# A fused joint network, forward and backward: another order for the row units and the second data gradient, and two gelu passes held behind the first GH product

## The chip, the cores and the metric

The kernel runs on one core of a Trainium2 chip. The metric is the device time of one execution in microseconds, the median of several runs. TensorE (PE in the profile) multiplies matrices and writes its results to PSUM; VectorE (DVE), ScalarE (ACT) and GpSimd (POOL) work on tiles in SBUF, the first two in PSUM too; SyncE (SP) and GpSimd issue the DMAs of this kernel. Each engine takes its instructions in the order of its own queue. An instruction whose input, or whose output buffer, is not yet free waits, and all that stand behind it in that queue wait with it.

## The reference

The forward pass is two convolutions of three taps with stride 2 and a gelu each, and then a joint network:

```python
h  = gelu(conv3(x,  w1))[:, ::2]        # x: (2, 16000, 256)
f  = gelu(conv3(h,  w2))[:, ::2]        # f: (2, 4000, 256)
j  = tanh((f @ w_f)[:, :, None] + (g @ w_g)[:, None])   # (2, 4000, 8, 256)
out = j @ w_o                           # (2, 4000, 8, 256)
```

All tensors are bfloat16. The kernel returns `out` and, for a given `grad_out` of the same shape, the gradients of `x`, `w1`, `w2`, `g`, `w_f`, `w_g` and `w_o`.

## The kernel before

The 4000 positions of both batch rows, with a gap between them, are laid side by side as 8016 columns and cut into 16 tiles of 512 columns, the last one shorter. For each tile `n` the outer loop runs four steps of the joint network, with two of the eight `u` in each. A step (`joint_units`, the "main" work) is, for each `u`: a square of the tanh on ScalarE (JSQ), matmuls of the output gradient with `w_o` (L623), and a VectorE pass on their result (NGZ, L627), which GpSimd adds up over the `u` (ACCN, L646); then blocks of output matmuls (L690), which ScalarE copies out (OUT, L692), alternating with matmuls of the gradient of `w_o` (L729).

Between the units of the main work, `weave` puts units of "fill" work, at a fixed ratio (0.92 fill units for each main unit). The fill is one chain of generators, written out by hand in the list `parts`. While tile `n` is in its joint steps, the fill holds the front of tile `n + 1` and the back of tile `n - 1`:

- `conv_units(n + 1)`: the first convolution, for even and for odd positions (L320), and the first four operations of each gelu: a square on ScalarE (`g_sq`), a VectorE pass (`g_s`, "the first pass" below), a sigmoid on ScalarE, and the VectorE product that writes HT. These four go into the queue `later`; `weave` takes two of them for each main unit (`pump`).
- `d1_units(n - 1)`: the gradient GF of the second gelu's input (L424, L426).
- `row_units(n - 1)`: five units, which transpose tiles on TensorE (L460) and copy them out (L462): first NGFE, copied by VectorE, and then four sets of HT and GF rows, copied by ScalarE. The next bullet's matmuls read them.
- `gwf_units` and `gw2_units(n - 1)`: the gradients of `w_f` (L506) and `w2` (L524) and their sums on VectorE (L408).
- `d5_units(n - 1)`: the data gradient of the second convolution, four units: two for even positions (two matmuls each, L447) and two for odd ones (four matmuls each). VectorE multiplies each result by G1 and writes GH (L450).
- then `ghr_units`, `conv2_units`, `e_units` and `fe_units`, which transpose GH, run the second convolution, form the gradients of `x` and `w1`, and start the next tile's joint network.

All matmul results and transposes of these units share one PSUM pool, `psp`, of 7 buffers. So a unit's matmuls wait until an engine has emptied the buffer that they are given. The order on each engine is made by the tile framework's scheduler from the order in which the units are issued, from its own estimates of time, and from dependencies added by hand. One of these is the list `held`: an operation that is put into `held` gets a dependency on the next GH product (L453), so that VectorE does it behind that product. Before, this held the last of the four gelu operations of the odd positions, for tiles `n > 1`; its line in the profile is L328.

Of the kernel before, what the change touches and what calls it, by code (L numbers as in the profile page):

```python
# [32 lines left out]
def kernel(  # L33
# [30 lines left out]
    def geom(n):  # L64
        c0 = n * CW
        return c0, min(CW, L - c0)
# [26 lines left out]
    def nsets(n):  # L93
        return 4 if geom(n)[1] == CW else 3

    def sets(n):
        s = nsets(n)
        return [(k, geom(n)[1] // s) for k in range(s)]
# [28 lines left out]
    def ps_f32():  # L127
        return psp.tile([P, 512], FP32, name="ps", tag="ps")
# [125 lines left out]
    held = []  # L254
    NOSYNC = mybir.DependencyInfo(mybir.DependencyClass.NoSync, mybir.DependencyReason.DATA)

    def pump(k):
        for _ in range(k):
            if later:
                later.popleft()()  # L260
# [37 lines left out]
    def conv_units(n):  # L298
        c0, W = geom(n)
        seconds = []  # L300
        st = S[n]
        HT = htp.tile([P, 2, KT, CW + 2], BF16, name="HT")
        G1 = g1p.tile([P, 2, KT, CW + 2], BF16, name="G1")
        st["HT"], st["G1"] = HT, G1
        if n == G - 1:
            nc.gpsimd.memset(G1[:, 0, :, 2 + W:3 + W], 0.0)
        if n == 0:
            nc.gpsimd.memset(HT[:, 1, :, 1:2], 0.0)
            nc.gpsimd.memset(G1[:, 1, :, 1:2], 0.0)
        else:  # L310
            nc.gpsimd.tensor_copy(out=HT[:, 1, :, 1:2], in_=S[n - 1]["HT"][:, 1, :, CW + 1:CW + 2])
        taps = {0: ((1, 0, 0), (2, 1, 0), (0, 3, -1)), 1: ((0, 1, 0), (2, 3, 0), (1, 2, 0))}
        for par in range(2):
            xb = gel.tile([P, KT, CW], BF16, name="g_x")
            for mt in range(KT):
                ps = ps_f32()
                k = 0
                for (i, c, sh) in taps[par]:
                    for kt in range(KT):
                        nc.tensor.matmul(ps[:, :W], lhsT=W1[:, i, kt, mt * P:(mt + 1) * P],  # L320
                                         rhs=st["X", c][:, kt, 16 + sh:16 + sh + W], start=(k == 0), stop=(k == 5))
                        k += 1
                nc.scalar.copy(out=xb[:, mt, :W], in_=ps[:, :W])  # L323
                yield
            first, second = gelu(xb, W, HT[:, par], G1[:, par], 2, HALVES if n == 0 else ((0, KT),))
            if par == 1 and n > 1:
                mult = first.pop()
                first.append(lambda: held.append(mult()))  # L328
            later.extend(first)
            seconds += second  # L330
            if n == 0:
                pump(len(first))
        seconds0.extend(seconds)
        if n > 0:
            seconds0.append(lambda: nc.gpsimd.tensor_copy(out=G1[:, 1, :, 1:2],
                                                          in_=S[n - 1]["G1"][:, 1, :, CW + 1:CW + 2]))
# [67 lines left out]
    def flush(key, acc, ps):  # L404
        if first_flush[key]:
            nc.vector.tensor_copy(out=acc, in_=ps)
        else:
            nc.vector.tensor_tensor(out=acc, in0=acc, in1=ps, op=ALU.add)  # L408
# [21 lines left out]
    def d5_units(n):  # L430
        st = S[n]
        c0, W = geom(n)
        N = W + 1 if n == G - 1 else W
        GF, G1 = st["GF"], st["G1"]
        GH = ghp.tile([P, 2, KT, CW + 4], BF16, name="GH")
        st["GH"] = GH
        if n == 0:
            nc.gpsimd.memset(GH[:, 0, :, 1:2], 0.0)
        else:
            nc.gpsimd.tensor_copy(out=GH[:, 0, :, 1:2], in_=S[n - 1]["GH"][:, 0, :, CW + 1:CW + 2])  # L440
        for par, taps in ((0, ((1, 0),)), (1, ((2, -1), (0, 0)))):
            for mt in range(KT):
                ps = ps_f32()
                k, last = 0, len(taps) * KT - 1
                for (i, sh) in taps:
                    for kt in range(KT):
                        nc.tensor.matmul(ps[:, :N], lhsT=W2T[:, i, kt, mt * P:(mt + 1) * P],  # L447
                                         rhs=GF[:, kt, 2 + sh:2 + sh + N], start=(k == 0), stop=(k == last))
                        k += 1
                gh = nc.vector.tensor_tensor(out=GH[:, par, mt, 2:2 + N], in0=ps[:, :N],  # L450
                                             in1=G1[:, par, mt, 2 - par:2 - par + N], op=ALU.mult)
                while held:
                    tc.add_manual_dep(held.pop().ins, gh.ins.name, NOSYNC, reason="held")  # L453
                yield
# [9 lines left out]
    def load_fr(n):  # L464
        W = geom(n)[1]
        FR = frp.tile([P, KT, 4, P], BF16, name="FR")
        nb = len(blocks(W))
        for kt in range(KT):
            nc.sync.dma_start_transpose(out=FR[:, kt, 0:nb, :], in_=S[n]["FT"][:, kt, 0:nb * P])
        S[n]["FR"] = FR  # L470
# [42 lines left out]
    def gw2_units(n):  # L513
        W = geom(n)[1]
        HG = S[n]["HG"]
        for i in (1, 2, 0):
            ps = ps_f32()
            for k, M in sets(n):
                for dt in range(KT):
                    if i == 0:  # L520
                        lhsT = HG[0][:M, 6 + dt, :] if k == 0 else HG[k - 1][:M, 2 + dt, :]
                    else:
                        lhsT = HG[k][:M, (0 if i == 1 else 2) + dt, :]
                    nc.tensor.matmul(ps[:, dt * D:(dt + 1) * D], lhsT=lhsT,  # L524
                                     rhs=HG[k][:M, 4:6, :].rearrange("p k d -> p (k d)"),
                                     start=(k == 0 and dt == 0), stop=(k == nsets(n) - 1 and dt == KT - 1))
            flush("2", ACC2[:, i, :], ps[:])
            yield
        first_flush["2"] = False

    def alternate(a, b):
        gens = [a, b]
        while gens:
            gen = gens.pop(0)
            if next(gen, StopIteration) is not StopIteration:
                gens.append(gen)
                yield
# [196 lines left out]
    def chain(*gens):  # L734
        for gen in gens:
            yield from gen

    def empty(k):
        for _ in range(k):
            yield  # L740
# [83 lines left out]
    for n in range(G):  # L824
        back, fwd = n > 0, n + 1 < G
        conv = conv_units(n + 1) if fwd else iter(())
        conv2 = conv2_units(n + 1) if fwd else iter(())
        late_open[0] = False
        parts = []
        if back:  # L830
            d1, e, rows, ghr = d1_units(n - 1), e_units(n - 1), row_units(n - 1), ghr_units(n - 1)
            parts += [islice(conv, 2), islice(d1, 1), islice(conv, 1), d1, conv, alternate(rows, d5_units(n - 1)),
                      gwf_units(n - 1), gw2_units(n - 1), islice(ghr, 1), islice(conv2, 1), ghr, conv2, islice(e, 6)]
            if fwd:
                parts.append(fe_units(n + 1))
            parts.append(e)
        else:
            parts += [conv, empty(3), islice(conv2, 1), empty(3), conv2, empty(3), fe_units(n + 1)]
        fill = chain(*parts)
        ratio = (0.92 if n > 0 else 0.4) if n + 1 < G else 0.72  # L840
        for up in range(U // 2):
            step = n * (U // 2) + up
            for i in range(2):
                if 2 * step + 4 + i < len(order):
                    load_got(*order[2 * step + 4 + i])
            if step + 1 < len(orderp):
                load_go(*orderp[step + 1])
            if up == 1:
                load_fr(n)
            if back and up < 2:  # L850
                load_xr(n - 1, 2 * up)
                load_xr(n - 1, 2 * up + 1)
            main = joint_units(n, up)
            weave(main, fill, ratio)
            if up == U // 2 - 1:
                for _ in fill:
                    pump(2)
                    pump_late(1)
                pump(len(later))
                late_open[0] = True  # L860
                pump_late(len(late))
            for i in range(2):
                if 2 * step + 2 + i < len(order):
                    tanh(*order[2 * step + 2 + i])
            if step + 1 < len(orderp):
                load_jr(*orderp[step + 1])
            if n + 2 < G:
                load_x(n + 2, ((0, 1, 3, 2)[up],))
    n = G - 1
# [79 lines left out]
```

## Time and profile before

| | |
|---|---|
| median of 3 runs | 850.34 us (848.83 to 851.24) |
| the profiled execution's own time | 843.12 us |
| its span in the profile | 841.4 us |
| PE busy | 812.8 us, 97% |
| ACT busy | 678.4 us, 81% |
| DVE busy | 620.3 us, 74% |
| POOL busy | 394.6 us, 47% |
| granted TensorE clock, mean | 0.994 |

In the rows of the profile, an engine's wait is written as the waiting instruction, an arrow, and the instruction that released it, then the total in us, how often, and the longest. A row of the timeline is the start in us from the span's start, the time taken, the engine, the line, the operation with its output and inputs, and in brackets the engine's idle time just before and what ended it. Instructions of one kind that follow each other are merged to one row with their count. Matmuls overlap: a group's time in the row is longer than the distance to the next group's start, so distances between starts are used for TensorE; and VectorE and ScalarE rows overlap by about 0.1 us with the next.

### The profile page before, as it was taken

Reading aid. Unit: us, or ns where it says so; the run is one execution under the profiler, and the core shown is the slowest. Engines: PE = TensorE matmul, PEld = TensorE weight load, DVE = VectorE, ACT = ScalarE, POOL = GpSimd, SP = SyncE. Lnnn points to the kernel's source line nnn. Section 1 sums busy time; section 2 is a strip of 40 time slices with the busy share of each in tenths; the row PEclk is TensorE's granted clock in tenths of the full one; section 3 lists DMA queues with packets and bytes.
Section 4 is the critical chain, followed back from the end, with each engine's and each line's share of the span. In section 5 each row is a group of like instructions: output and inputs, shape, how many; then the busy total and the mean of one; then the engine's idle time right before and its main releaser. Section 6 shows DMA issues by size and latency. Waiting matters only on the chain.

```text
span 841.4 us, 17055 instructions
## 1 busy us (share of the span) xinstructions
PE 812.8 (97%) x6396; PEld 598.2 (71%) x6396; DVE 620.3 (74%) x1217; ACT 678.4 (81%) x1080; POOL 394.6 (47%) x423
## 2 busy tenths in 40 slices
PE   7969999999999999999999999999999999999997
PEld 3546677767768677676766777677686776878796
DVE  4896696876778767697866968768687676967644
ACT  3889998796978969699796987969789696987744
POOL 1154544444534535444486644445345354445661
PEclk9999999999999999999999999999999999999999
DMA  9988999999999999999999999999999999999954
GB/s 188 194 198 182 212 229 233 216 251 235 225 221 259 226 229 245 243 222 183 224 255 210 233 233 228 251 210 265 238 237 264 210 227 231 220 210 228 243 157 135
DMA packets 398515, 187.21 MB, mean 223 GB/s; under 512 B 346464, under 2 KB 382200, under 8 KB 398432
## 3 DMA queue, kind: packets, MB, share of 16 engines
q1 hardware_dynamic: 378112, 119.00, 77.9%
q0 software_dynamic: 20320, 67.12, 27.5%
q8 instruction: 50, 0.82, 0.4%
q14 instruction: 33, 0.27, 0.1%
HBM read 51.38 MB, written 50.34 MB: 121 GB/s over the span
## 4 chain that ended last, share of the span: by engine, by line
PE 43%; ACT 41%; DVE 6%; issue 5%; DMA 4%; POOL 0%; SPq 0%; ACTq 0%; POOLq 0%; DVEq 0%
ACT JT L396 12%; PE ps L593 7%; ACT OUT L692 6%; ACT JSQ L617 6%; PE GWO_ps L729 6%; PE ps L580 6%; PE ps L690 6%; ACT rows L462 5%; PE ps L355 5%; PE ps L524 4%; PE ps L623 4%; ACT g_s L260 3%; ACT g_x L323 3%; PE pst L460 2%; ACT GX L583 2%
## 5 line engine op out<-in xcount | busy, mean ns | idle before, releaser
L646 POOL TENSOR_TENSOR ACCN<-ACCN,NGZ 128x1024 f32<-128x1024 f32 (+1 forms) x80 | 168.7, 2109 | 69.1 <-DVE NGZ L627 68.0
L627 DVE SCALAR_TENSOR_TENSOR NGZ<-JSQ,ps 128x512 bf16<-128x512 bf16 (+3 forms) x272 | 167.5, 640 | 43.2 <-PE ps L623 39.9
L692 ACT CAST OUT<-ps 128x512 bf16<-128x512 f32 (+1 forms) x252 | 148.4, 600 | 58.4 <-PE ps L690 58.2
L396 ACT ACTIVATE JT<-FE,GE 128x512 bf16<-128x512 f32 (+3 forms) x272 | 182.3, 711 | 4.0 <-PE ps L623 1.9
L617 ACT ACTIVATE JSQ<-JT 128x1024 bf16<-128x1024 bf16 (+1 forms) x128 | 135.8, 1064 | 25.6 <-DVE NGZ L627 25.6
L729 PE MATMUL GWO_ps<-GO,JR 128*128 128x256 bf16 (+1 forms) x1008 | 148.6, 273 | 2.1 <-DVE JR L462 2.1
L690 PE MATMUL ps<-WO,JT 128*128 128x256 bf16 (+1 forms) x1008 | 148.7, 274 | 0.3 <-ACT rows L462 0.3
L717 POOL DMA_DIRECT2D out_dram<-OUT x76 | 55.8, 735 | 184.4 <-ACT OUT L692 171.5
L623 PE MATMUL ps<-GOT,WOT 128*128 128x512 bf16 (+1 forms) x512 | 139.2, 376 | 0.8 <-DVE rows L462 0.8
L260 DVE SCALAR_TENSOR_TENSOR g_s<-g_sq,g_x 128x1024 bf16<-128x1024 bf16 (+2 forms) x49 | 81.2, 1657 | 50.1 <-ACT g_sq L260 50.1
L729 PEld LDWEIGHTS <-JR 128*128 128x128 bf16 (+1 forms) x1008 | 96.9, 98 | 28.6 <-DVE JR L462 2.4
L690 PEld LDWEIGHTS <-JT 128*128 128x128 bf16 (+1 forms) x1008 | 97.9, 98 | 22.1 <-issue 1.6
L580 PE MATMUL ps<-W1T,GH 128*128 128x256 bf16 (+2 forms) x756 | 100.4, 273 | 0.0
L408 DVE TENSOR_TENSOR ACC<-ACC,ps 128x512 f32<-128x512 f32 x90 | 61.5, 684 | 44.5 <-PE ps L524 32.8
L580 PEld LDWEIGHTS <-GH 128*128 128x128 bf16 (+2 forms) x756 | 83.5, 116 | 13.0
L320 PE MATMUL ps<-XC,W 128*128 128x512 bf16 (+1 forms) x384 | 91.3, 375 | 1.1 <-DMA XC<-in_x_dram 1.1
L593 PE MATMUL ps<-rows,XR 128*128 128x256 bf16 (+1 forms) x756 | 90.4, 273 | 0.0
L593 PEld LDWEIGHTS <-XR 128*128 128x128 bf16 (+1 forms) x756 | 74.0, 98 | 11.6
L583 ACT CAST GX<-ps 128x512 bf16<-128x512 f32 (+2 forms) x126 | 72.2, 587 | 10.5 <-DMA out_dram<-GX 4.1
L241 POOL DMA_DIRECT2D out_dram<-GX x67 | 36.7, 548 | 82.1 <-ACT GX L583 75.0
L623 PEld LDWEIGHTS <-WOT 128*128 128x128 bf16 x512 | 48.5, 98 | 33.6 <-issue 2.3
L320 PEld LDWEIGHTS <-W 128*128 128x128 bf16 x384 | 37.4, 98 | 38.5 <-issue 1.4
(131 smaller groups left out, 1214.2 us busy)
## 6 DMA issues: line engine op xcount, KB each, us to landing
GO<-in_grad_out_dram SPq DMA_DIRECT2D x56, 512.0 KB, 5.3
out_dram<-OUT POOLq DMA_DIRECT2D x56, 512.0 KB, 5.5
out_dram<-GX POOLq DMA_DIRECT2D x55, 256.0 KB, 4.3
XR<-in_x_dram POOLq DMA_DIRECT2D x39, 256.0 KB, 6.3
XR<-in_x_dram POOLq DMA_DIRECT2D x13, 320.0 KB, 6.2
GOT<-in_grad_out_dram SPq DMA_TRANSPOSE x136, 5.7
JR<-JT SPq DMA_TRANSPOSE x128, 4.8
GO<-in_grad_out_dram SPq DMA_DIRECT2D x4, 384.0 KB, 5.0
```

What stands on the lines that cost most here:

```text
L260: later.popleft()()
L320: nc.tensor.matmul(ps[:, :W], lhsT=W1[:, i, kt, mt * P:(mt + 1) * P], rhs=st["X", c][:, kt, 16 + sh:16 + sh + W], start=(k == 0), stop=(k ...
L396: nc.scalar.activation(out=JT[:, mt, lo:hi], in_=S[n]["FE"][:, mt, lo:hi], func=ACT.Tanh, bias=GE[:, b, mt, u:u + 1], scale=1.0)
L580: nc.tensor.matmul(ps[:M, cj * D:(cj + 1) * D], lhsT=GH[:, par, kt, o:o + s * (M - 1) + 1:s], rhs=W1T[:, i, kt, :], start=(j == 0), stop=( ...
L593: nc.tensor.matmul(ps[:, dt * D:(dt + 1) * D], lhsT=XR[:M, 4 * k + i + 2 * (1 - par), dt * P:(dt + 1) * P], rhs=t[:M, g + 2 * par:g + 2 * ...
L617: nc.scalar.activation(out=JSQ[:, :, :W], in_=JT[:, :, :W], func=ACT.Square)
L623: nc.tensor.matmul(ps[:, :W], lhsT=WOT[:, kt, mt * P:(mt + 1) * P], rhs=GOT[:, kt, :W], start=(kt == 0), stop=(kt == KT - 1))
L627: nc.vector.scalar_tensor_tensor(out=NGZ[:, mt, lo:hi], in0=JSQ[:, mt, lo:hi], scalar=1.0, in1=ps[:, lo:hi], op0=ALU.subtract, op1=ALU.mul ...
L646: st["last"] = nc.gpsimd.tensor_tensor(out=out, in0=in0, in1=st["NGZ", u][:, :, :W], op=ALU.add)
L690: nc.tensor.matmul(ps[:M, j * V:(j + 1) * V], lhsT=st["JT", u][:, kt, o:o + M], rhs=WO[:, kt, :], start=(kt == 0), stop=(kt == KT - 1))
L692: nc.scalar.copy(out=OUT[:M, k, :], in_=ps[:M, :])
L729: nc.tensor.matmul(GWO_ps[:, dt, :], lhsT=JR[:M, j, dt, k, :], rhs=GO[:M, k, j * V:(j + 1) * V], start=(n_gwo[0] == 0), stop=(n_gwo[0] == ...
```

## The change

The change has two parts. Inside the loop, `alternate(rows, d5)` issues the row units R and the units D of the data gradient in turn: R D R D R D R D R. The new function `braid` issues R D R D R D R R D: the last set of rows now comes before the last unit of the data gradient. The call behind the loop, for the last tile, still uses `alternate`.

The second part is in the odd positions' gelu: of the four operations, the second (the first VectorE pass) and the fourth (the product that writes HT) are put into `held`, where before only the fourth was. Both appear as L328 in the changed kernel. Lines from `alternate` on are 4 higher there.

```diff
@@ conv_units
             if par == 1 and n > 1:
-                mult = first.pop()
-                first.append(lambda: held.append(mult()))
+                for j in (1, 3):
+                    first[j] = partial(lambda f: held.append(f()), first[j])
             later.extend(first)
@@ behind gw2_units
+    def braid(rows, d5):
+        for gen in (rows, d5, rows, d5, rows, d5, rows, rows, d5):
+            yield next(gen, None)
+
@@ the loop over tiles
-            parts += [islice(conv, 2), islice(d1, 1), islice(conv, 1), d1, conv, alternate(rows, d5_units(n - 1)),
+            parts += [islice(conv, 2), islice(d1, 1), islice(conv, 1), d1, conv, braid(rows, d5_units(n - 1)),
                       gwf_units(n - 1), gw2_units(n - 1), islice(ghr, 1), islice(conv2, 1), ghr, conv2, islice(e, 6)]
```

## The prediction

> **What bounds the kernel now.** I read the page's first part, then TensorE's longest waits, then the busy time of each engine inside one tile, and last the timeline of the stretch where TensorE stands still.
>
> ```profile
> span 841.4 us, 17055 instructions
> PE 812.8 (97%) x6396; PEld 598.2 (71%) x6396; DVE 620.3 (74%) x1217; ACT 678.4 (81%) x1080; POOL 394.6 (47%) x423
> ```
> ```profile
> PE ps L524 <- ACT rows L462: 5.3, 13, 0.7
> PE ps L447 <- DVE GH L450: 3.9, 11, 0.7
> ```
> ```profile
> core 0: us, PE busy (x) PEld busy (x) DVE busy (x) ACT busy (x) POOL busy (x), PEclk, DMA share, GB/s
> 335.04:346.20 11.16, 10.49 (x89) 7.28 (x87) 8.75 (x18) 11.13 (x16) 6.08 (x7) 1.00 1.06 263
> 346.30:385.80 39.50, 39.50 (x309) 29.61 (x307) 30.72 (x68) 31.17 (x59) 17.01 (x18) 1.00 1.12 212
> ```
>
> TensorE is the bound. Only two waits recur on it once per tile, and both lie in the stage that the change edits. The windows are one tile period: the stage (335.04 to 346.20) has 0.67 us without matmuls, the rest of the period none; there PE is busy 39.50 of 39.50 us at full clock. In the stage ScalarE is busy 11.13 of 11.16 us, so there ScalarE, not TensorE, may set the pace. What can be won lies in these stages, and what is won there is kept, since nothing outside them is late.
>
> The stage on TensorE. I call the four GH matmul groups D1 to D4 (L447), the transposes of the four row sets R1 to R4 (L460), their ScalarE copies by the same names, and the next two output blocks O1 and O2 (L690):
>
> ```profile
> 338.00 1.03 PE L623 MATMUL ps<-GOT,WOT 128*128 128x512 bf16 x4
> 339.29 1.03 PE L447 MATMUL ps<-GF,W2T 128*128 128x512 bf16 x4 [0.26 <-DVE GH L450]
> 340.15 0.59 PE L623 MATMUL ps<-GOT,WOT 128*128 128x512 bf16 x2
> 340.58 0.39 PE L460 MATMUL pst<-ident,HT 128*128 128x128 bf16 x4
> ...
> 340.92 0.59 PE L623 MATMUL ps<-GOT,WOT 128*128 128x512 bf16 x2
> 341.35 1.03 PE L447 MATMUL ps<-GF,W2T 128*128 128x512 bf16 x4
> 342.22 0.60 PE L690 MATMUL ps<-WO,JT 128*128 128x256 bf16 x4
> ...
> 343.43 1.04 PE L506 MATMUL ps<-rows,FR 128*128 128x256 bf16 x8
> 344.30 0.60 PE L729 MATMUL GWO_ps<-GO,JR 128*128 128x256 bf16 x4
> 344.74 0.82 PE L524 MATMUL ps<-rows 128*128 128x256 bf16 x6
> 345.97 0.39 PE L524 MATMUL ps<-rows 128*128 128x256 bf16 x2 [0.41 <-ACT rows L462]
> ```
>
> From start to start, four 128x512 matmuls cost 0.87 (341.35 to 342.22), two 0.43, a row set's six transposes 0.34 (340.58 to 340.92), four 128x256 matmuls 0.44 (344.30 to 344.74). So D3 (339.29) could have begun at 338.00 + 0.87 = 338.87: lost 0.42. The last pair of the W2 gradient (345.97) could have begun at 344.74 + 6 x 0.11 = 345.39: lost 0.58. The two other engines:
>
> ```profile
> 336.45 0.68 DVE L462 COPY rows<-pst 128x1024 bf16<-128x1024 bf16 x1
> 337.40 1.23 DVE L260 SCALAR_TENSOR_TENSOR g_s<-g_sq,g_x 128x1024 bf16<-128x1024 bf16 x1 [0.28 <-ACT g_sq L260]
> 338.55 1.28 DVE L450 TENSOR_TENSOR GH<-ps,G 128x512 bf16<-128x512 f32 x2
> 339.93 0.69 DVE L328 TENSOR_TENSOR HT<-g_s,g_x 128x1024 bf16<-128x1024 bf16 x1
> 340.54 0.68 DVE L627 SCALAR_TENSOR_TENSOR NGZ<-JSQ,ps 128x512 bf16<-128x512 bf16 x1
> ```
> ```profile
> 338.83 1.06 ACT L260 ACTIVATE g_s<-g_s 128x1024 bf16<-128x1024 bf16 x1
> 339.79 1.71 ACT L462 COPY rows<-pst 128x1024 bf16<-128x1024 bf16 x2
> ...
> 342.94 0.81 ACT L462 COPY rows<-pst 128x768 bf16<-128x768 bf16 x1
> 343.68 1.06 ACT L617 ACTIVATE JSQ<-JT 128x1024 bf16<-128x1024 bf16 x1
> 344.64 0.57 ACT L692 CAST OUT<-ps 128x512 bf16<-128x512 f32 x1
> 345.11 0.80 ACT L462 COPY rows<-pst 128x768 bf16<-128x768 bf16 x1
> ```
>
> D3 waits because its PSUM buffer is the one that the first GH product empties; that product stands behind the odd gelu's first VectorE pass (337.40 to 338.63) and ends at 338.55 + 0.68 = 339.23, 0.06 before D3. The last pair waits for the copy R4, which ends at 345.91 because it stands behind a square (343.68) and an output copy (344.64).
>
> **The change part by part.** No instruction is added or removed; this is all order. In the built program TensorE's order differs in 15 stages (R4 and D4 change places around O1), VectorE's in 11 stages (the other four have the first GH product ahead already, or no odd gelu), ScalarE's in the same places. Every SyncE instruction stays in place. On GpSimd a two-column HT copy moves one place forward, in front of one add; no DMA is passed.
>
> (1) The first pass behind GH1. VectorE after the row copy (a pass costs 0.60 from start to start, the gelu's first pass 1.15, HT 0.61): GH1 337.05 to 337.73, first pass 337.65 to 338.88, GH2 338.80 to 339.48, first NGZ 339.40 to 340.08. D3 then starts unheld at 338.87, a gain of 0.42. What waits behind the first pass is the sigmoid on ScalarE; in the built order the copy R1 now goes first, at 338.83, so the sigmoid finds its input ready. Sigmoid and R1 change places and R2 ends at 341.50 as before; it starts 0.81 earlier, at 340.69, and the sigmoid ends about 340.79.
>
> (2) The product HT is now between the two NGZ passes. It is held by the sigmoid: 340.83 to 341.52, second NGZ 341.44 to 342.12, GH3 from 342.04. Before, that NGZ ended at 341.82. Behind HT in VectorE's queue are the second NGZ, GH3, two more NGZ and GH4, and TensorE waits for their PSUM buffers.
>
> (3) R4 before D4. On ScalarE R3 stays at 342.94, R4 follows at 343.68 and ends 344.49 instead of 345.91; the output copy and the square come after it. The square's reader is far off, so it costs nothing there:
>
> ```profile
> 353.13 0.68 DVE L627 SCALAR_TENSOR_TENSOR NGZ<-JSQ,ps 128x512 bf16<-128x512 bf16 x1
> ```
>
> TensorE after: D3 338.87, NGZ matmuls 339.74, R3 340.17, NGZ matmuls 340.51, R4 340.94, and O1 could go at 341.28. But O1's buffer is now the one that R2's copy empties: 341.50 + 0.06 = 341.56, lost 0.28. D4 could follow at 342.00; its buffer is freed by the second NGZ, 342.12 + 0.06 = 342.18, lost 0.18. Then O2 343.05 (GH3 is out at 342.72), L506 343.49, L729 344.36, L524 344.80, last pair 345.45, with R4 ready for 0.96. Against 345.97 the stage wins 0.52 of the 1.00 it loses now; the other half turns into the two new waits.
>
> The sum: 11 stages x 0.52 = 5.7. In the three others that have an odd gelu only R4's step counts; nothing shows it exactly, it lies between 0 and 0.58, and I take 0.4, nearer the upper end since their R4 copy is late in the same way: 1.2. The fifteenth, the one without an odd gelu, counts 0: the two waits have 11 and 13 rows for 15 stages. Together 6.9. The profiled execution took 843.12 us (span 841.4): it becomes 836.2. It ran 7.2 below the median of 850.34, and I take the same 6.9 off the median: **843.4**. Ends of the unknown: nothing won, 850.3; everything won, 11 x 0.42 + 13 x 0.58 = 12.2, 838.1.
>
> **The rivals.** Less than 0.3% (2.6 us) can't be told from no change here.
>
> *Both waits vanish whole: 838.1.* It needs R2's copy to end before 341.22 and the second NGZ before 341.66. For it: ScalarE may come into the stage earlier than before, if TensorE delivers earlier. Against it: ScalarE has no slack in the stage (11.13 of 11.16).
>
> *The first pass runs beside a GpSimd add: no change.* Its cost is in the trace:
>
> ```profile
> 306.28 2.12 POOL L646 TENSOR_TENSOR ACCN<-ACCN,NGZ 128x1024 f32<-128x1024 f32 x1 [0.33 <-DVE NGZ L627]
> ...
> 306.76 2.73 DVE L260 SCALAR_TENSOR_TENSOR g_s<-g_sq,g_x 128x1024 bf16<-128x1024 bf16 x1 [0.62 <-ACT g_sq L260]
> ```
>
> There the add ran till 308.40 and the same pass took 2.73 instead of 1.23. In the stage it would end at 340.38, the sigmoid at 341.48, HT at 342.21, the second NGZ at 342.81, and D4 would start at 342.87 instead of 342.18: the stage would end at 346.14, 0.17 worse than before, 11 x 0.17 - 1.2 = +0.7: 851.0. Against it, the adds around the stage:
>
> ```profile
> 330.01 2.12 POOL L646 TENSOR_TENSOR ACCN<-NGZ 128x1024 f32<-128x1024 bf16 x1 [1.34 <-DVE NGZ L627]
> ...
> 341.99 2.13 POOL L646 TENSOR_TENSOR ACCN<-ACCN,NGZ 128x1024 f32<-128x1024 f32 x1 [0.90 <-DVE NGZ L627]
> ```
>
> No add runs from 332.13 to 341.99, and the pass moves by 0.25. The Trainium skill, "SBUF — State Buffer", section "Who interferes with whom", states this as a rule: a VectorE instruction with two SBUF inputs and a GpSimd one that reads SBUF take the shared port in turn, and the later one is blocked until the first is done. The trace agrees: 306.76 + 2.73 = 309.49 is the add's end plus 1.09.
>
> *Slower: HT is caught by an add.* Its row shows 0.69 as a rule and 2.02 once:
>
> ```profile
> L260 DVE TENSOR_TENSOR HT<-g_s,g_x x20: 413/692/2023, 13.7 to 743.2; 128x1024 bf16<-128x1024 bf16 x15, 128x512 bf16<-128x512 bf16 x4, 128x672 bf16<-128x672 bf16 x1
> ```
>
> If an add is under way at 340.83, the second NGZ and D4 slip by 1.33, the last pair comes at 346.78, 0.81 later than now: 11 x 0.81 - 1.2 = +7.7, 858.0. It decides once HT ends more than 0.5 later than worked out. Against it: the add now waits for the second NGZ, which stands behind HT, and the one before ends at 332.13.
>
> *The change gives nothing, since a later stage waits for ScalarE or GpSimd instead: 850.* Against it: behind the stage TensorE is busy 39.50 of 39.50 us while ScalarE is idle for 8.3.
>
> **How the numbers follow.** Forecast 0.67, both waits gone 0.12, the first pass beside an add 0.07, nothing won 0.06, HT caught 0.08. The range leaves out the slower case and half of the full win: 838 to 850.5. Faster by over 0.3%: the first two without a tail of the forecast under 2.6 us, 0.77; within 0.3%: 0.14; slower: 0.09.
>
> **What would show it.** In the profile after, the wait of L447 for GH and that of L524 for ScalarE's rows are gone or nearly; in their place O1 (L694) waits some 0.1 to 0.3 for ScalarE's rows and L447 as much for VectorE's NGZ, about 11 times each; HT (L328) waits 0.7 for the sigmoid; the copy R4 follows R3 directly; the tile period falls from 50.8 by 0.5. I am wrong if the first pass takes over 1.3 us, if HT takes over 0.8, if ScalarE reaches R1 at another time than 3.8 us behind D1 (here 338.83 against 335.04, where the first window begins), or if TensorE has new waits outside the stage.

## The result, and the profile after

The change made the kernel faster: 841.4 us against 846.8 us, medians of 22 runs each, and a ratio of 0.9917 with a 95% interval of 0.989 to 0.9944. The ratios, here and below, compare the fast runs of each kernel alone, those within 1.5% of its fastest; the medians over all runs lie 5.4 us apart here and 2.6 and 2.2 us in the two later measurements. The prediction was 843.4 from 850.34, a ratio of 0.9918; its 850.34 was the median of three runs of the kernel before, 22 runs gave 846.8, so the gains are to be compared and not the times. Two later measurements of the same kernel, each with its own runs of the kernel before, gave 0.9958 (0.9924 to 0.9992) and 0.9945 (0.9907 to 0.9983), so by the ratios the gain lies between some 3.6 and 7 us.

The page's first lines for the changed kernel:

```profile
span 843.6 us, 17055 instructions
PE 816.5 (97%) x6396; PEld 600.8 (71%) x6396; DVE 619.7 (73%) x1217; ACT 679.8 (81%) x1080; POOL 393.8 (47%) x423
```

This profiled execution took 845.37 us and shows no gain over the profiled one of before (843.12). Where it lost time is seen when the span is cut at the first GH matmuls (D1) of consecutive tiles. The columns are the stretch, its length, then busy time and instructions of each engine, the granted clock, the DMA share and GB/s:

```profile
333.74:383.99 50.25, 50.09 (x397) 37.10 (x395) 39.36 (x86) 42.48 (x74) 23.15 (x24) 1.00 1.12 224
383.99:437.82 53.83, 50.63 (x396) 36.84 (x394) 36.71 (x95) 43.93 (x75) 32.68 (x36) 1.00 1.10 217
437.82:491.61 53.79, 51.59 (x396) 38.07 (x394) 40.72 (x71) 43.57 (x68) 29.57 (x34) 0.97 1.15 229
491.61:545.30 53.69, 50.75 (x397) 37.03 (x395) 38.71 (x70) 43.25 (x68) 23.16 (x23) 1.00 1.15 224
```

The same tile of the kernel before, and the longest of its three tiles in the middle:

```profile
335.04:385.81 50.77, 50.10 (x396) 36.99 (x394) 39.47 (x86) 42.41 (x74) 23.19 (x24) 1.00 1.10 223
...
436.57:489.52 52.95, 50.41 (x396) 37.03 (x394) 40.90 (x71) 43.90 (x69) 32.01 (x36) 1.00 1.14 227
```

So a tile that nothing disturbs takes 50.25 us instead of 50.77, 0.52 less. The three tiles in the middle took 10.6 more than three times 50.25 in this profile, and 6.8 and 7.9 more in the two later ones; in the profile of before the excess was 2.2. Two other tiles of this profile are longer too, 51.45 and 51.97 for those from 230.32 to 333.74. I come back to this below. From here on kernels are compared by an undisturbed tile, D1 to the next tile's D1, which repeats to 0.03 us between runs of one kernel, and by the ratio.

The edited stage of that tile and the rest of it, changed kernel:

```profile
333.74:344.38 10.64, 10.48 (x89) 7.42 (x87) 8.64 (x18) 10.55 (x15) 5.25 (x8) 1.00 1.06 198
344.38:383.99 39.61, 39.61 (x311) 29.69 (x309) 30.72 (x68) 31.93 (x60) 17.90 (x17) 1.00 1.13 231
```

As before, TensorE is busy all the time outside the stage (39.61 of 39.61); the stage went from 11.16 to 10.64. TensorE in the stage:

```profile
337.56 1.03 PE L447 MATMUL ps<-GF,W2T 128*128 128x512 bf16 x4
...
339.63 0.39 PE L460 MATMUL pst<-ident,HT 128*128 128x128 bf16 x4
339.85 0.28 PE L460 MATMUL pst<-ident,GF 128*128 128x128 bf16 x2
340.24 0.60 PE L694 MATMUL ps<-WO,JT 128*128 128x256 bf16 x4
340.88 1.03 PE L447 MATMUL ps<-GF,W2T 128*128 128x512 bf16 x4
...
343.49 1.04 PE L524 MATMUL ps<-rows 128*128 128x256 bf16 x8
```

D3 (337.56) and the eight matmuls of L524 (343.49, in one row now) run unheld. O1 (340.24) comes 0.27 after the end of R4's 0.34 (339.63 + 0.34 = 339.97), and D4 (340.88) 0.20 after O1's 0.44. These are the two new waits. The rows carry no bracket for them: idle time in brackets counts from the modelled end of the matmul before, some 0.16 after its successor could have started, so a wait of 0.2 vanishes there. In the list of waits therefore O1 shows only four times, and D4's wait for the NGZ pass not at all:

```profile
PE ps L694 <- ACT rows L462: 1.4, 4, 0.4
```

VectorE and ScalarE in the stage:

```profile
336.33 1.22 DVE L328 SCALAR_TENSOR_TENSOR g_s<-g_sq,g_x 128x1024 bf16<-128x1024 bf16 x1
...
339.53 0.69 DVE L328 TENSOR_TENSOR HT<-g_s,g_x 128x1024 bf16<-128x1024 bf16 x1 [0.78 <-ACT g_s L260]
340.14 0.68 DVE L631 SCALAR_TENSOR_TENSOR NGZ<-JSQ,ps 128x512 bf16<-128x512 bf16 x1
```
```profile
337.52 1.02 ACT L462 COPY rows<-pst 128x1024 bf16<-128x1024 bf16 x1
338.42 1.08 ACT L260 ACTIVATE g_s<-g_s 128x1024 bf16<-128x1024 bf16 x1
339.38 0.81 ACT L462 COPY rows<-pst 128x768 bf16<-128x768 bf16 x1
340.06 0.75 ACT L396 ACTIVATE JT<-FE,GE 128x512 bf16<-128x512 f32 x1
340.86 1.06 ACT L621 ACTIVATE JSQ<-JT 128x1024 bf16<-128x1024 bf16 x1
341.82 1.48 ACT L462 COPY rows<-pst 128x768 bf16<-128x768 bf16 x2
```

R2's copy ends at 340.19 and O1 starts 0.05 later; the second NGZ ends at 340.82 and D4 starts 0.06 later. The copies R3 and R4 are one row (341.82, x2): R4 follows R3 directly, ahead of the output copy and the square, and ends at 343.30, 0.85 before the last pair of L524 needs it (343.49 + 6 x 0.11 = 344.15).

### The profile page after: what moved, and what is told of

Read it like the earlier page. It is cut to its first block, busy times and chain, and to the rows that moved or that the text cites. A ratio compares the mean times of both kernels' runs of the same rounds, so it can differ in the third digit from the quotient of the medians.

```text
span 843.6 us, 17055 instructions
## 1 busy us (share of the span) xinstructions
PE 816.5 (97%) x6396; PEld 600.8 (71%) x6396; DVE 619.7 (73%) x1217; ACT 679.8 (81%) x1080; POOL 393.8 (47%) x423
## 4 chain that ended last, share of the span: by engine, by line
PE 71%; ACT 15%; DMA 6%; DVE 6%; issue 2%; ACTq 0%
PE GWO_ps L733 10%; PE ps L694 9%; PE ps L627 8%; PE ps L597 8%; PE ps L584 7%; DMA JR<-JT 6%; PE ps L524 5%; PE ps L320 5%; PE ps L355 4%; PE pst L460 4%; ACT JT L396 4%; PE ps L447 4%; ACT JSQ L621 2%; ACT OUT L696 2%; DVE NGZ L631 2%
## 5 line engine op out<-in xcount | busy, mean ns | idle before, releaser
L733 PE MATMUL GWO_ps<-GO,JR 128*128 128x256 bf16 (+1 forms) x1008 | 150.8, 274 | 5.9 <-DMA JR<-JT 3.8
L260 DVE SCALAR_TENSOR_TENSOR g_s<-g_sq,g_x 128x1024 bf16<-128x1024 bf16 (+2 forms) x35 | 65.7, 1876 | 47.8 <-ACT g_sq L260 47.8
L587 ACT CAST GX<-ps 128x512 bf16<-128x512 f32 (+2 forms) x126 | 72.2, 586 | 10.6 <-PE ps L584 4.8
```

Of the source, the lines that this page charges most:

```text
L587: nc.scalar.copy(out=t[:M, 2 * cp:2 * cp + 2, :], in_=ps[:M, :])
L733: nc.tensor.matmul(GWO_ps[:, dt, :], lhsT=JR[:M, j, dt, k, :], rhs=GO[:M, k, j * V:(j + 1) * V], start=(n_gwo[0] == 0), stop=(n_gwo[0] == ...
```

## The experiments

The theory after the result: two causes, each half of it. The hold frees D3 from the first pass (0.42), the other order brings R4's copy ahead of the square (0.58), and 0.48 of the two comes back as the waits of O1 and D4. The main rival: only one of the two matters. They are told apart by doing one at a time.

**The change itself again**, as the measure for the others:

> The changed kernel itself, run again beside the versions that split it. If the reading of its profile is right, a tile away from the batch seam takes 50.25 us (before: 50.77), O1 waits 0.28 for ScalarE's copy R2 and D4 0.18 for the second NGZ, and neither D3 nor the last pair of the W2 gradient waits. Time about 0.992 of before.

Ratio 0.9958 (0.9924 to 0.9992), undisturbed tile 50.25 us. That is the tile of the first profile.

**The hold alone**: the rows and the second data gradient in their old order.

```diff
-            parts += [islice(conv, 2), islice(d1, 1), islice(conv, 1), d1, conv, braid(rows, d5_units(n - 1)),
+            parts += [islice(conv, 2), islice(d1, 1), islice(conv, 1), d1, conv, alternate(rows, d5_units(n - 1)),
```

> Only the second part: the first pass is held behind GH1, the units alternate as before. Theory A (a chain of bounds, the last of them R4's copy): D3 starts unheld, 0.42 earlier, but R4 stays behind the square and the output copy on ScalarE and ends 10.9 after D1, so the last pair waits about 1.0 instead of 0.58 and the stage wins 0.0: tile period 50.77, ratio 1.000. Theory B (each part takes away its own wait and the gains add up): the tile gets shorter by 0.42, period 50.35, ratio 0.994.

Ratio 1.0024 (0.9991 to 1.0057). An undisturbed tile, TensorE's longest wait, and two NGZ passes on VectorE and then ScalarE in the stage:

```profile
284.39:335.47 51.08, 50.27 (x397) 37.04 (x395) 38.14 (x69) 42.60 (x67) 23.18 (x24) 1.00 1.14 234
```
```profile
PE ps L524 <- ACT rows L462: 9.1, 13, 0.8
```
```profile
290.80 0.68 DVE L631 SCALAR_TENSOR_TENSOR NGZ<-JSQ,ps 128x512 bf16<-128x512 bf16 x1
...
292.61 0.68 DVE L631 SCALAR_TENSOR_TENSOR NGZ<-JSQ,ps 128x512 bf16<-128x512 bf16 x1
```
```profile
291.52 1.06 ACT L621 ACTIVATE JSQ<-JT 128x1024 bf16<-128x1024 bf16 x1
...
293.33 1.06 ACT L621 ACTIVATE JSQ<-JT 128x1024 bf16<-128x1024 bf16 x1
294.30 0.57 ACT L696 CAST OUT<-ps 128x512 bf16<-128x512 f32 x1
294.76 0.80 ACT L462 COPY rows<-pst 128x768 bf16<-128x768 bf16 x1
```

The tile takes 51.08, 0.31 more than before. D3's wait is gone, but the last pair of L524 now waits 9.1 us in all instead of 5.3. R4's copy still stands behind the square (293.33) and the output copy, and it ends 0.30 later after D1 than before (295.56 - 284.39 = 11.17 against 345.91 - 335.04 = 10.87). The squares are later (293.33 is 8.94 after D1; before it was 343.68 - 335.04 = 8.64): they write one of two JSQ buffers, which the NGZ passes free, and the product HT, held by the sigmoid, now delays those passes. Each of the two squares starts 0.04 after the end of an NGZ pass (290.80 + 0.68 = 291.48 and 291.52; 292.61 + 0.68 = 293.29 and 293.33). So taking away the wait of D3 gained nothing by itself. The expectation was no change; it's slightly worse, by a coupling that I had not worked out.

**The other order alone**: the hold as it was before, for the product only.

```diff
-                for j in (1, 3):
-                    first[j] = partial(lambda f: held.append(f()), first[j])
+                mult = first.pop()
+                first.append(lambda: held.append(mult()))
```

> Only the first part: R4 before D4, the first pass where it was. Theory A: D3 still waits 0.42 for GH1, but R4 follows R3 on ScalarE and is out 9.4 after D1, O1 finds R2 done, D4 finds the second NGZ done, and the last pair starts 10.36 after D1 without a wait: the stage wins 0.57, as much as both parts together (0.52) or a little more; tile period 50.20, ratio 0.991. Theory B: only its own wait goes, 0.58, and both parts would have to give 1.0, which the changed kernel doesn't show; if the hold is what brings the gain, the period stays at 50.77.

Ratio 0.9928 (0.9885 to 0.9972), tile 50.18. The tile, TensorE's longest wait, and the copies R3 and R4:

```profile
281.22:331.40 50.18, 49.93 (x397) 37.09 (x394) 38.34 (x69) 42.38 (x67) 23.16 (x24) 1.00 1.11 236
```
```profile
PE ps L447 <- DVE GH L450: 4.0, 11, 0.7
```
```profile
289.12 1.51 ACT L462 COPY rows<-pst 128x768 bf16<-128x768 bf16 x2
```

R4's copy again follows R3's directly. Here D3 waits its 0.42 as before the change, and everything behind it runs unheld. That is the whole gain and 0.07 more: with the hold the stage loses 0.47 (O1 and D4), without it 0.42 (D3). Measured again beside the change:

> The other order of the units alone, with the product of the odd positions' gelu where it was before the change: 50.18 us for an undisturbed tile, 0.07 less than with the hold, so a ratio within 0.002 of the change's. Were the hold worth the 0.42 that the prediction gave it, this kernel would stand 4.6 us (0.5 per cent) behind the change.

> The change itself once more beside it: 50.25 us for an undisturbed tile and a ratio of about 0.992.

Ratios 0.9949 (0.9905 to 0.9994) and 0.9945 (0.9907 to 0.9983), tiles 50.21 and 50.25. Beside the other order, the hold is worth nothing that can be measured in the ratio, and 0.04 to 0.07 us a tile in the wrong direction.

**R4's place in ScalarE's queue alone.** If the order on TensorE doesn't matter in itself, then the kernel before, with nothing changed but that the square of the step's second `u` is put behind R4's copy, must show the gain too (`copied` is the copy that `transposes` issues last):

```diff
+            if k == 3:
+                r4.append(copied)
...
-        nc.scalar.activation(out=JSQ[:, :, :W], in_=JT[:, :, :W], func=ACT.Square)
+        sq = nc.scalar.activation(out=JSQ[:, :, :W], in_=JT[:, :, :W], func=ACT.Square)
+        if u % 2 and r4:
+            tc.add_manual_dep(sq.ins, r4.pop().ins.name, NOSYNC, reason="square behind the rows")
```

> The kernel before with one thing changed: the square of the next step's second u is held behind the copy R4 on ScalarE. Units alternate as before, nothing is held on VectorE beyond the old product. If ScalarE's queue is the cause, R4 is out 9.9 after D1, the last pair doesn't wait (10.35 after D1), D3 waits 0.42 as before, and the period is 50.19, ratio 0.991, as with R4 before D4. If TensorE's new order is needed, the period stays at 50.77.

Ratio 0.9923 (0.9883 to 0.9962). An undisturbed tile, TensorE's longest wait, and ScalarE:

```profile
181.47:231.66 50.19, 49.92 (x396) 37.06 (x394) 38.41 (x71) 42.41 (x67) 23.16 (x24) 1.00 1.16 230
```
```profile
PE ps L448 <- DVE GH L451: 3.7, 11, 0.7
```
```profile
189.38 0.81 ACT L463 COPY rows<-pst 128x768 bf16<-128x768 bf16 x1
190.06 0.62 ACT L698 CAST OUT<-ps 128x512 bf16<-128x512 f32 x1
190.54 0.85 ACT L463 COPY rows<-pst 128x768 bf16<-128x768 bf16 x1
...
191.71 1.12 ACT L621 ACTIVATE JSQ<-JT 128x1024 bf16<-128x1024 bf16 x1
```

TensorE's and VectorE's order are those of before, R4's copy (190.54) comes one square earlier, and the tile takes 50.19. The wait of L524 is gone, that of D3 stays.

**And the reverse**: the change, with R4's copy held behind that square.

```diff
+            if k == 3 and n < G - 1:
+                held4.append(copied)
...
+        while u % 2 and held4:
+            tc.add_manual_dep(held4.pop().ins, sq.ins.name, NOSYNC, reason="held")
```

> The changed kernel, TensorE's and VectorE's order untouched, but ScalarE makes the copy R4 only behind the output copy of O1 and the square, where it stood before. If the place in ScalarE's queue is what the gain hangs on, R4 is out 10.9 after D1 again, the last pair waits about 0.5, and the period is back at 50.77, ratio 1.000. If the earlier transposes on TensorE are what brings it, the period stays at 50.25, ratio 0.992.

Ratio 1.0037 (1.0006 to 1.0069).

```profile
284.90:335.82 50.92, 50.25 (x396) 37.04 (x394) 38.25 (x69) 42.51 (x67) 23.13 (x24) 1.00 1.11 231
```
```profile
PE ps L528 <- ACT rows L463: 8.4, 14, 1.7
```
```profile
294.17 1.07 ACT L625 ACTIVATE JSQ<-JT 128x1024 bf16<-128x1024 bf16 x1
295.12 0.80 ACT L463 COPY rows<-pst 128x768 bf16<-128x768 bf16 x1
```

The tile takes 50.92, against 50.25, and the last pair waits for R4 again. It is 0.15 more than the expected 50.77: the waits of O1 and D4 are still there, beside R4's. The four runs together settle the cause of the tile's gain: R4's copy ahead of the square is enough for it, and without it the gain is gone.

**Taking away the two new waits.** O1 waits for R2's copy, since the sigmoid stands ahead of it on ScalarE, and D4 for the second NGZ, since HT stands ahead of it on VectorE. Three kernels move these. In the first HT is held behind GH3; in the second the sigmoid is held behind R2's copy as well; in the third HT is held only behind the second NGZ:

```diff
-                for j in (1, 3):
-                    first[j] = partial(lambda f: held.append(f()), first[j])
+                first[1] = partial(lambda f: held.append(f()), first[1])
+                first[3] = partial(lambda f: held3.append(f()), first[3])
...
+                while par == 1 and held3:
+                    tc.add_manual_dep(held3.pop().ins, gh.ins.name, NOSYNC, reason="held")
```

The second kernel has these lines besides (`copied` is again the copy of a row set):

```diff
+                first[2] = partial(lambda f: heldsig.append(f()), first[2])
...
+            while k == 1 and heldsig:
+                tc.add_manual_dep(heldsig.pop().ins, copied.ins.name, NOSYNC, reason="held")
```

The third has a list `held2` in the place of `held3`, and empties it behind the NGZ pass instead of GH:

```diff
+            while mt == 1 and held2:
+                tc.add_manual_dep(held2.pop().ins, ngz.ins.name, NOSYNC, reason="held")
```

> The changed kernel with HT held behind the third GH product instead of the first, the sigmoid where it was. If D4's wait of 0.18 comes from HT standing before the second NGZ, it goes, and O1's wait of 0.28 for R2 stays: last pair 10.23 after D1, tile period 50.07, ratio 0.990. If D4 waits for something else, the period stays at 50.25.

> The changed kernel with two more holds: the sigmoid of the odd gelu behind R2's copy on ScalarE, and HT behind the third GH product on VectorE. Theory A: R2 is out about 5.6 after D1 and the second NGZ about 5.7, so neither O1 nor D4 waits, R4 is out 9.4 after D1, and the last pair starts 9.95 after D1: the stage loses nothing, 1.0 less than before; tile period 49.8, ratio 0.985. Rival: the late sigmoid and HT (about 7.2 after D1 instead of 6.5) hold up something behind them on VectorE or the second convolution, and the period stays at 50.25 or rises; ratio 0.992 or more.

> The changed kernel with HT held one place later only: behind the second NGZ, in front of the third GH product. Behind that product HT took 2.6 us and cost TensorE 1.0 per tile. Theory A (HT was caught there by GpSimd's add, which started 0.09 before it): one place further up HT starts about 5.8 after D1, before the add (6.07), takes 0.69, and the add waits for HT instead; D4 finds the second NGZ done, only O1's wait of 0.28 is left; tile period 50.07, ratio 0.989. Rival (any place behind the second NGZ costs TensorE the VectorE time of HT): HT's time falls on GH3 and the later passes, and the period stays near 51.2.

All three missed: ratios 1.0055 (1.0019 to 1.0091), 1.0103 (1.0063 to 1.0143) and 1.0078 (1.0039 to 1.0117), tiles 51.22, 51.22 and 51.80. The waits that they aimed at did go: in the first and the third D4 follows O1 after 0.43, in the second O1 has no wait either (6.23 after D1, where R4's transposes end). What came in their place is longer, counted from start to start: the gradient of `w_f` waits for an NGZ pass, 1.17 in the first and 1.45 in the second, and O2 for a GH product, 1.59 in the third. The second and third expectation had named a rival of this size, the third with another cause. The same thing happened in each. HT behind GH3, and the GpSimd add beside it:

```profile
290.81 2.61 DVE L329 TENSOR_TENSOR HT<-g_s,g_x 128x1024 bf16<-128x1024 bf16 x1
```
```profile
290.71 2.14 POOL L653 TENSOR_TENSOR ACCN<-ACCN,NGZ 128x1024 f32<-128x1024 f32 x1
```

With the sigmoid behind R2's copy too:

```profile
290.94 1.64 DVE L331 TENSOR_TENSOR HT<-g_s,g_x 128x1024 bf16<-128x1024 bf16 x1 [0.88 <-ACT g_s L330]
```
```profile
289.88 2.14 POOL L658 TENSOR_TENSOR ACCN<-ACCN,NGZ 128x1024 f32<-128x1024 f32 x1
```

HT behind the second NGZ, with TensorE's wait that follows from it:

```profile
290.17 2.95 DVE L329 TENSOR_TENSOR HT<-g_s,g_x 128x1024 bf16<-128x1024 bf16 x1 [0.17 <-ACT g_s L261]
```
```profile
290.42 2.14 POOL L653 TENSOR_TENSOR ACCN<-ACCN,NGZ 128x1024 f32<-128x1024 f32 x1
```
```profile
PE ps L697 <- DVE GH L451: 12.9, 9, 1.4
```

HT takes 0.69 when nothing is beside it. Here it ends 0.56 to 0.57 after the end of the add in all three (293.42 against 292.85, 292.58 against 292.02, 293.12 against 292.56). The add needs the second NGZ. In the change HT stands ahead of that NGZ, so the add can't run yet:

```profile
340.98 2.13 POOL L650 TENSOR_TENSOR ACCN<-ACCN,NGZ 128x1024 f32<-128x1024 f32 x1 [1.21 <-DVE NGZ L631]
```

Held behind it, HT meets the add, which in all three kernels starts 6.05 to 6.06 after D1, right behind DMA issues on GpSimd. In the third kernel the next GH product and with it O2 (L697) come late.

**HT behind the second NGZ, and early enough.** The last kernel keeps that hold and takes R2's copy off ScalarE, so that what follows the sigmoid on ScalarE moves up and one more VectorE instruction stands ahead of the second NGZ:

```diff
-            transposes(srcs, [(t[:M, 0:len(srcs)], M, 0, len(srcs))], nc.scalar.copy)
+            transposes(srcs, [(t[:M, 0:len(srcs)], M, 0, len(srcs))], nc.vector.tensor_copy if k == 1 and n < G - 1 else nc.scalar.copy)
```

> As before, and the copy R2 moved from ScalarE to VectorE, behind the second GH product, where VectorE idles 0.75 per tile before HT. If O1's wait of 0.28 comes from ScalarE's queue in front of R2, it goes too: R2 is out about 5 after D1; HT starts about 6.15, still before the add; what is left is at most 0.15 at the w_f gradient for R3 or the third NGZ. Tile period 49.8 to 49.95, ratio 0.984 to 0.987, the fastest of all. Rival: the longer VectorE queue puts HT behind the add's start, HT takes 2.6 again and the period is near 51.

Ratio 0.9886 (0.9812 to 0.996, six runs). The tile, then HT with the copy R2 before it, and the add:

```profile
279.79:329.65 49.86, 49.86 (x396) 37.08 (x394) 38.63 (x70) 41.68 (x66) 23.46 (x24) 1.00 1.14 240
```
```profile
284.12 0.55 DVE L463 COPY rows<-pst 128x768 bf16<-128x768 bf16 x1
...
285.79 0.69 DVE L329 TENSOR_TENSOR HT<-g_s,g_x 128x1024 bf16<-128x1024 bf16 x1
```
```profile
286.03 2.44 POOL L653 TENSOR_TENSOR ACCN<-ACCN,NGZ 128x1024 f32<-128x1024 f32 x1 [0.20 <-DVE NGZ L632]
```

The sigmoid is done when VectorE reaches HT, so HT goes without a wait; it takes 0.69, and now the add is the one that takes longer, 2.44 instead of 2.13. In the whole tile TensorE is busy 49.86 of 49.86 us: both waits of the change are gone, 0.39 a tile (a wait of 0.10 ahead of L506 is left, too short to show as idle time). Measured again, beside the third measurement of the change:

> The same kernel as ht_ngz2_r2_vector, run again beside the change itself. If its gain over the change is real, an undisturbed tile again takes about 49.86 us against the change's 50.25, which is 11 x 0.39 = 4.3 us less: a ratio to before of about 0.987 with the change at 0.992. Rival: the first measurement caught quiet runs and the two ratios agree within 0.002.

Ratio 0.9931 (0.9887 to 0.9974) against the change's 0.9945, tile 49.86 again. The tile's gain over the change repeats. Over the whole run the two can't be told apart: the ratios agree within 0.002, which is what the rival said. This version is faster than before by both measurements, and faster than the change by the tile alone. It also shows what the hold can be worth: here D3 doesn't wait, behind it only the 0.10 ahead of L506 is left, and the tile is 0.32 to 0.35 shorter than with the other order alone (50.18 and 50.21). How much of that is the hold, and how much the two other moves, no run separates.

**What stays open.** The extra time of the three middle tiles. In profiles of the change it was 10.6, 6.8 and 7.9 us, in the one of before 2.2, with the other order alone 2.1 both times, with the hold alone 3.8, and with R2's copy on VectorE 4.2 and 7.1. That looks as if the hold beside the other order made them worse, but the ratios of the change and of the other order alone don't differ, and the square behind R4, which holds no more than before, showed extra time in its middle tiles as well (50.87, 51.68, 52.83 and 56.77 against 50.19). A part of it is TensorE waiting for the DMA that writes JR: 3.8 us over the whole run in the first profile of the change, 1.5 and 2.1 in the two others, 3.4 with the square behind R4, and none in the profile of before. Why that DMA comes late, and what the rest is, I haven't tested.

## Why the prediction was right

Its steps against the changed kernel's profile, in us from the start of D1 (335.04 in the profile of before, 333.74 after):

| step | worked out | measured |
|---|---|---|
| (1) D3 starts unheld | 3.83 | 3.82 |
| (1) R1's copy ahead of the sigmoid | 3.79 | 3.78 |
| (2) HT, held by the sigmoid | 5.79 to 6.48 | 5.79 to 6.48 |
| (2) D4, held by the second NGZ | 7.14 | 7.14 |
| (3) O1, held by R2's copy | 6.52 | 6.50 |
| (3) R4's copy ends | 9.45 | 9.56 |
| (3) last pair of L524 | 10.41 | 10.41 |

- *The sum.* Each stage was to win 0.52; the undisturbed tile went from 50.77 to 50.25. For the three stages with only R4's step I took 0.4 each, at most 0.58. Two of them can be read: the first tile went from 50.94 to 50.17 and the last but one from 42.35 to 41.99, so they won 0.77, more than the bound (its last pair had waited 0.84, not 0.58), and 0.36; the third lies in the middle tiles. The twelve tiles between these two would make 6.2 at 0.52, together 7.4 against the 6.9 predicted, if nothing disturbed them. The extra time of the middle tiles is a term that the sum doesn't have.
- *The number.* The first measurement says 7.0 (0.0083 x 846.8), the later ones 3.6 and 4.6. So the stage is explained, but that the first ratio, 0.9917, meets the forecast 0.9918 so closely is luck; the difference between the measurements may lie in the middle tiles.
- *Step (1), "a gain of 0.42", is true of D3 and not of the stage.* The hold alone gained nothing (51.08), and without the hold nothing was lost (50.18). D3's wait lay on TensorE's path in front of a later one, and each wait removed let the next one grow: TensorE came earlier to a buffer or a copy that was not ready earlier. The stage came out right because the prediction did not add up gains, but followed TensorE through the new order to the last pair, with what each engine had ready at that time.
- *Step (2)* is right to 0.01, and it is what the hold costs: 0.78 of idle time in front of HT, which the passes behind it, and D4, take over.
- *Step (3)* is the whole gain. R4's copy ended 0.11 later than worked out, because the square ahead of R3 waited for a JSQ buffer (the same coupling that made the hold alone slower); R4 was still ready 0.85 early.
- *Both waits vanish:* not here; R2's copy ended at 6.45 and the second NGZ at 7.08. HT behind the second NGZ, together with R2's copy on VectorE, did it, 0.39 a tile.
- *The first pass beside an add:* the pass took 1.22, no add near it.
- *HT caught by an add:* this did not happen in the change, but it did in three of the four kernels that put HT behind the second NGZ. Its price there was 0.97, 0.97 and 1.55 a tile over the change; the prediction had 1.33 (0.81 + 0.52). Its point of decision, "HT ends more than 0.5 later", was not the right one: while HT stands ahead of the second NGZ, a later HT delays the add too.
- *The gain given back later:* not in undisturbed tiles, where TensorE is busy 39.61 of 39.61 behind the stage. The sign of being wrong that the prediction names, new waits of TensorE outside the stage, does show in some of the other tiles: the waits for the DMA that writes JR.

## What to carry to other kernels

Where one engine loses time at two places of a stage, the gains of removing them don't add: walk the engine through the new order to the last place, with what the others have ready, and then ask which of the two edits is needed; here one moved ScalarE instruction was the whole gain and the other edit, beside it, nothing. Before an instruction is moved on VectorE, look at what the instruction in front of it releases on GpSimd: an order that looks late can be what keeps two of them apart. Short waits of TensorE are found in the distances between starts, not in its idle time.

## What the runs showed of the hardware

With HT behind the second NGZ, HT's row starts 0.25 us before the add's (290.17 against 290.42), and HT is still held for the whole add (2.95 instead of 0.69). With R2's copy on VectorE, HT's row again starts 0.24 before the add's (285.79 against 286.03), and there HT goes first and the add is lengthened by 0.30. The Trainium skill, "SBUF — State Buffer", section "Who interferes with whom", says that whoever issues first gets the shared port for the whole instruction. The runs agree that one of the two is held by the other (HT ended 0.56 to 0.57 after the add in three kernels, the add took 0.30 longer in the fourth), but the order of the rows doesn't tell which. In the first case HT had waited 0.17 for the sigmoid and the add stood right behind DMA issues on GpSimd; in the second HT had not waited and the add had. Whether it is this that decides, or only that GpSimd's row starts are rough, is not settled.
